# Diagonal blocks of short pairs transposed by the DMA, attention's steps at two places of a unit

## The chip, the cores and the metric

One core of one Trainium2 chip runs the whole program. The metric is the device time of one execution in microseconds (us), as the median of several runs. TensorE does the matmuls, VectorE (DVE) and ScalarE (ACT) the elementwise work, GpSimd (POOL) some scaling and subtraction, and SyncE (SP) issues the DMAs.

## What is computed

```python
# q, k, v: B, H, S, D = 4, 8, 576, 64; all fp32
scores = where(causal, -1e9, q @ k.T / sqrt(D))
local = softmax(scores) @ v
q_p = phi(q)                                  # where(q > 0, q, exp(q) - 1) + 1
mem_out = (q_p @ M_prev) / (q_p @ z_prev + 1e-6)
attn = g * mem_out + (1 - g) * local          # g = sigmoid(beta), one per head
x = attn as [2304 tokens, 512]
h = x @ w_in;  x = (h * sigmoid(1.702 * h)) @ w_out          # layer 0, d_ff = 2048
h = x @ w_in2; x = (h * clip(h + 3, 0, 6) / 6) @ w_out2      # layer 1
```

## The kernel before

Tokens are taken in six tiles of 384 (`TILES`). Four hold the first 384 rows of one batch ("long"), and two hold the last 192 rows of two batches each ("short"): the third and the sixth. Attention works on pairs of heads. A long tile has 4 pairs; a short one has 8, because it holds two batches. Pairs 0 to 7 belong to the first two tiles. From pair `CROSS` = 8 on (third tile and later) the softmax weights are transposed by the DMA and not by TensorE.

The mixture-of-experts layers (MoE) run as a stream of units, one for each of 16 blocks of d_ff. A unit has four quarters of h (`moe`, three matmuls of 384 columns each: L390, L392, L393) and then four quarters of y of the unit before (L361 to L363). So it has eight quarters, and after each the main loop counts `qi` up by one. While tile `ti` runs through layer 0, attention for tile `ti` + 1 is mixed in: attention is a generator, and `pump` (L1018; it is called at the end of the main loop) asks it for as many steps as the count allows. In h there is one PSUM bank (in layer 0), so a unit's first h matmul waits until the gate of the unit before (ACT at L327, DVE at L329) has read it.

A step of a short pair `i` is one of these: the first scores (`scores`, 2 banks), the memory term (`mem_read`, 1 bank), three steps of `turn(i - 1)`, the second scores "s4, s5" for rows 128 to 191 (2 banks), and `weigh(i - 1)`, which multiplies with v into o (1 bank). Attention has a rotation of three PSUM banks (`bank`). Scores go through a DVE minimum (L531), an ACT exponential (L536), a DVE reciprocal (L540) and a POOL scaling (L544). `over` then copies the weights as two 16-bit halves on ACT (L580), and SP issues a DMA transpose (L586) from `sp` to `xp`. `turn` starts `join`s: DVE copies (L605) that put the halves together into `pt`. The last 64 columns of a short pair, the diagonal block `t2`, are the exception: TensorE transposes them (t4b, L485), DVE copies the result from PSUM to `t4` (L705), and `weigh` reads `t4` last.

Instructions are put in order by a planner. It goes by what it believes to be ready, and by program order among those. `issue_after` ties an instruction behind another of its engine. The h matmuls are tied only behind attention's TensorE work of `SLACK` = 10 steps earlier. `later` lets a copy of `over` wait until a new gate's ACT cast has been written out, for up to `MOST` = 16 steps of the chains; at most two copies follow one gate.

The pace is `PG1` = 0.78: in a short tile 57 steps are spread over 0.78 * 128 quarters, one step every 1.75 quarters.

Of the kernel before, what the change touches and what calls it, by code (L numbers as in the profile page):

```python
# [11 lines left out]
U16 = mybir.dt.uint16  # L12
# [13 lines left out]
KQ = 39  # L26
CR = 8.5
OFF = 3
PG0 = (0.85, 0.8)
PG1 = 0.78  # L30
TB = 3
PB = 6
RB = 3
# [27 lines left out]
WAIT = (3, 5)  # L61
PB2, SB2, XB2, PTB2 = 4, 2, (4, 3), 2
APART = 2
MOST = 16
S2 = 104
SR = 8
CONV2 = tuple(range(4, 110, 13)) + tuple(range(140, 210, 10))
# [45 lines left out]
def attention_moe_kernel(ctx: ExitStack, tc: tile.TileContext, qk0, sk0, sk1, vm0, vm1, bb, w1, w2, out):  # L113
# [370 lines left out]
    def at_transpose(*args):  # L484
        on_pe[:] = [PE.transpose(*args).ins]  # L485

    def attention(ap, room, across):
# [84 lines left out]
        def over(i, a, src, n, blocks):  # L572
# [13 lines left out]
            SP.dma_start_transpose(out=turned, in_=halves[:, 0:2 * n])  # L586
            joins.setdefault(i, []).append((a, blocks, turned))

        def join(i, a, blocks, turned):

            yield
            t = heads(i)
            v = turned.rearrange("p (h b) q -> p h b q", h=2)
            if a is None:
                jobs = [(t[k][:, :, 128:192], v[:, :, :, 64 * k:64 * k + 64]) for k in range(2)]
            elif pairs[i][3] == 1:
                jobs = [(t[a][:, :, 0:128], v)]
            else:
                jobs = [
                    (t[a][:, to:to + 128 * (b1 - b0)].rearrange("p (b q) -> p b q", q=128), v[:, :, b0:b1])  # L600
                    for b0, b1, to in blocks
                ]
            for out, w in jobs:
                with tc.issue_after(gated["DVE"][-1]):
                    d = DVE.tensor_copy(out=out.bitcast(U16).rearrange("p b (q h) -> p h b q", h=2), in_=w)  # L605
                made.setdefault(i, {})[DVE] = d.ins

        def scores(i):

            ti, si, b, g, p, _ = pairs[i]  # L610
            norms[1] = ti
            q, k = qk[i]
            st = ap.tile([128, 12], F32, tag="st", name="st")
            mx, su = st[:, 0:6], st[:, 6:12]

            def product(banks, blocks):

                mm = in_a_run(free(banks[0]) + free(banks[1]))
                for o0, o1, c0 in blocks:
                    for a in range(2):  # L620
                        h = slice(64 * a, 64 * a + 64)
                        mm(
                            banks[a][:, o0:o1], lhsT=q[h, c0:c0 + 128], rhs=k[h, 0:o1 - o0], start=True, stop=True
                        )

            def soft(s, cols, dst, c):

                jobs = [(a, c0, c1, c + a * len(cols) + x) for a in range(2) for x, (c0, c1) in enumerate(cols)]
                yield
                for a, c0, c1, k in jobs:  # L630
                    masked_min(s[a][:, c0:c1], mask[:, 512 - (c1 - c0):512], BIG, mx[:, k:k + 1])
                yield
                for a, c0, c1, k in jobs:
                    d = expo(dst[a][:, c0:c1], s[a][:, c0:c1], mx[:, k:k + 1], su[:, k:k + 1])
                    if c1 == cols[-1][1]:
                        has_read(s[a], d)
                yield
                inverse(su[:, c:c + len(jobs)])
                yield
                for a, c0, c1, k in jobs:  # L640
                    norm(dst[a][:, c0:c1], su[:, k:k + 1], omg[:, 2 * p + a:2 * p + a + 1])
                if i >= CROSS:
                    yield
                    for a in range(2):
                        yield from over(i, a, dst[a], *merges0[g][c > 0])

            pp[i] = []
            if g == 0:
                parts = (((0, 128, 0), (128, 384, 128)), ((0, 384, 256),))
            else:  # L650
                parts = (((0, 512, 0),),)
            def weights(a):
                return room[0].tile([128, 512], F32, tag="p", bufs=PB2 if i >= CROSS else PB, name="p")

            t = [[None if i >= CROSS else weights(a) for _ in parts] for a in range(2)]
            pp[i] = [tuple(x) for x in t]
            c = 0
            for x, blocks in enumerate(parts):
                s = [bank("s") for _ in range(2)]
                if i >= CROSS:  # L660
                    for a in range(2):
                        t[a][x] = weights(a)
                product(s, blocks)
                start(("s", i, x), soft(s, [(o0, o1) for o0, o1, _ in blocks], [t[a][x] for a in range(2)], c))
                c += 2 * len(blocks)
                yield
            if g == 1:
                t = room[0].tile([128, 512], F32, tag="p", bufs=PB2 if i >= CROSS else PB, name="p4")
                t2 = ap.tile([128, 64], F32, tag="p5", name="p5")
                pp[i].append((t, t2))  # L670
                s, s2 = bank("s4"), bank("s5")
                mm = in_a_run(free(s) + free(s2))
                for o, c0, c1 in ((s, 0, 512), (s2[:, 0:64], 512, 576)):
                    for a in range(2):
                        h = slice(64 * a, 64 * a + 64)
                        mm(o[h], lhsT=q[h, 128:N1], rhs=k[h, c0:c1], start=True, stop=True)

                def soft4(s=s, s2=s2, t=t, t2=t2):
                    yield
                    masked_min(s, mask[:, 0:1].to_broadcast([128, 512]), BIG, mx[:, 2:3])  # L680
                    masked_min(s2[:, 0:64], mask4, mx[:, 2:3], mx[:, 3:4])
                    yield
                    has_read(s, expo(t, s, mx[:, 3:4], su[:, 2:3]))
                    has_read(s2, expo(t2, s2[:, 0:64], mx[:, 3:4], su[:, 3:4]))
                    yield
                    DVE.tensor_tensor(out=su[:, 2:3], in0=su[:, 2:3], in1=su[:, 3:4], op=ALU.add)
                    inverse(su[:, 2:3])
                    yield
                    norm(t, su[:, 2:3], omp[:, p:p + 1])
                    norm(t2, su[:, 2:3], omp[:, p:p + 1])  # L690
                    if i >= CROSS:
                        yield
                        yield from over(i, None, t, 512, [(0, 4, None)])

                start(("s", i, 2), soft4())
                yield
# [13 lines left out]
        def turn(i):  # L710
            ti, si, b, g, p, _ = pairs[i]
            if i >= CROSS:
                need(("s", i, 0), ("s", i, 1), ("s", i, 2))
                for k in (0, 1, None):
                    if k is not None:
                        head(i)
                    for n, (a, blocks, turned) in enumerate(joins[i]):
                        if a == k:
                            start(("j", i, n), join(i, a, blocks, turned))
                    if k == 1 and g == 1:  # L720
                        ps2 = bank("t4b")
                        at_transpose(ps2[0:64, 0:128], pp[i][2][1], ident)
                        start(
                            ("t", i, 0, 1),
                            evac(i, [(DVE, t4[0:64], ps2[0:64, 0:128].rearrange("p (a c) -> p a c", a=2), ps2)]),
                        )
                    yield
                if g == 0:
                    yield
# [100 lines left out]
        def weigh(i):  # L830

            ti, si, b, g, p, last = pairs[i]
            v = vm.pop(i)[0]
            need(*[("j", i, n) for n in range(4)])
            need(("t", i, 0, 0), ("t", i, 0, 1), ("t", i, 1, 0), ("t", i, 1, 1), ("m", i))
            t = pt.pop(i)
            o = bank("o")
# [111 lines left out]
        for i in range(CROSS, NPAIR):  # L949
            s = scores(i)  # L950
            if i == CROSS or pairs[i - 1][5]:
                yield from chunks(s, 1)
                yield from pause(2)
                yield from chunks(s, 9)
                begun(i)
            else:
                t, w = turn(i - 1), weigh(i - 1)
                yield from chunks(s, 1)
                yield from mem_read(i - 1)
                load_qk(i + 1)  # L960
                for gen, n in ((t, 1), (s, 1), (t, 1), (s, 9), (t, 9)):
                    yield from chunks(gen, n)
                begun(i)
                yield from chunks(w, 9)
            if pairs[i][5]:
                yield from pause(WAIT[pairs[i][3]])
                yield from mem_read(i)
                load_qk(i + 2)
                yield from ended(i, turn(i), weigh(i))


    with ExitStack():
# [80 lines left out]
        with tc.tile_pool(name="ap", bufs=2) as ap, ExitStack() as second, ExitStack() as third:  # L1053
# [28 lines left out]
            for layer, t, f in stream:  # L1082
# [8 lines left out]
                    convert_to(min(NF, PRE + 1 + int(qi / CR)))  # L1091
                if ti < 2 and 128 * ti + qi >= S2:
                    part_to(1 + (128 * ti + qi - S2) // SR)
                pump((qi - OFF) / (PG0[min(ti, 1)] * 128 / 36 if TILES[ti + 1][0][1] == 0 else PG1 * 128 / 57))

        with tc.tile_pool(name="x2p", bufs=2) as x2p:
            state["pool"] = x2p
# [68 lines left out]
```

## Time and profile before

| what | value |
|---|---|
| median of 3 runs | 1037.05 us (1036.7 to 1039.19) |
| the profiled execution | 1035.5 us |
| its span, first to last instruction | 1033.7 us |
| TensorE busy | 97% of the span |
| DVE, ACT, POOL busy | 49%, 53%, 30% |
| layer 0 of tile 2 with attention for the third tile (short) | 157.0 to 278.6 us |
| layer 0 of tile 3 with attention for the fourth tile (long) | 278.6 to 367.5 us |
| layer 0 of tile 5 with attention for the sixth tile (short) | 455.1 to 578.5 us |

The stage bounds are those of the copies of y at the end of each tile (L413). Engine times are busy times; a gap on TensorE of over 0.15 us counts as idle, and its releaser is inferred from the semaphores.

### The profile page before, as it was taken

How to read it: one execution, taken by the hardware profiler on the slowest of the kernel's cores; microseconds unless marked ns; L12 is line 12 of the kernel's file. 1: busy time of each engine (PE TensorE's matmuls, PEld its weight loads, DVE VectorE, ACT ScalarE, POOL GpSimd, SP SyncE). 2: the span in 40 equal slices, each digit the busy share in tenths (PEclk: the TensorE clock that was granted, in tenths of full speed). 3: DMA queues.
4: the chain of work that ended last, by engine and by line, in shares of the span. 5: the costliest groups of instructions: out<-in, count | busy, mean ns of one | idle time of the engine just before them, and what ended most of it. 6: DMA issues, size and time to landing. Idle time of an engine off the chain costs nothing.

```text
span 1033.7 us, 15855 instructions
## 1 busy us (share of the span) xinstructions
PE 999.3 (97%) x5737; PEld 884.3 (86%) x5737; DVE 507.1 (49%) x1263; ACT 552.7 (53%) x1142; POOL 309.8 (30%) x346
## 2 busy tenths in 40 slices
PE   7899999979999999999989999999999999999998
PEld 5556558767888888887868999999999999999998
DVE  6987775677554446346554887861121211211110
ACT  5877767656655365365554987963232332323322
POOL 3522013434344244233332331232222222222221
PEclk9999999999999999999999999999999999999999
DMA  5844418765454044236644774010010000100000
GB/s 176 308 160 166 155 62 204 183 154 125 119 95 97 16 111 82 70 77 124 123 97 101 298 272 145 1 31 32 1 62 1 31 31 1 47 16 1 32 1 31
DMA packets 110175, 99.15 MB, mean 96 GB/s; under 512 B 80400, under 2 KB 89616, under 8 KB 110096
## 3 DMA queue, kind: packets, MB, share of 16 engines
q1 hardware_dynamic: 110096, 98.14, 33.8%
q8 instruction: 45, 0.74, 0.3%
q14 instruction: 34, 0.28, 0.1%
HBM read 61.41 MB, written 9.44 MB: 69 GB/s over the span
## 4 chain that ended last, share of the span: by engine, by line
PE 67%; DVE 5%; DMA 4%; ACT 3%; issue 2%; POOL 1%; ACTq 0%; DVEq 0%; POOLq 0%; SPq 0%
PE h L390 11%; PE h L392 10%; PE h L393 10%; PE y L361 10%; PE y L363 10%; PE y L362 10%; DMA xp<-sp 3%; PE o L470 3%; PE s L470 2%; ACT p L536 1%; DVE pt L605 1%; DVE s L531 1%; ACT sp L580 1%; DVE w L274 1%; POOL p L544 1%
## 5 line engine op out<-in xcount | busy, mean ns | idle before, releaser
L341 POOL TENSOR_TENSOR g<-t,g 128x384 fp32r<-128x384 f32 x173 | 185.7, 1074 | 482.6 <-ACT g L338 369.5
L390 PE MATMUL h<-xs,w 128*128 128x384 f32 x704 | 243.1, 345 | 9.3 <-DVE t L329 9.1
L392 PE MATMUL h<-xs,w 128*128 128x384 f32 x704 | 236.9, 336 | 0.2 <-DVE w L274 0.2
L393 PE MATMUL h<-xs,w 128*128 128x384 f32 x704 | 236.7, 337 | 0.0
L361 PE MATMUL y<-g,w 128*128 128x384 f32 x704 | 236.5, 336 | 0.0
L362 PE MATMUL y<-g,w 128*128 128x384 f32 x704 | 236.2, 335 | 0.0
L363 PE MATMUL y<-g,w 128*128 128x384 f32 x704 | 221.2, 337 | 0.0
L333 DVE SCALAR_TENSOR_TENSOR t<-t,h 128x384 f32<-128x384 f32 x96 | 53.1, 553 | 278.6 <-ACT t L331 278.5
L544 POOL TENSOR_SCALAR p<-p,st,omg 128x128 f32<-128x128 f32 (+3 forms) x128 | 95.9, 760 | 198.4 <-DVE st L540 100.4
L390 PEld LDWEIGHTS h<-xs,w 128*128 128x128 f32 x704 | 132.7, 189 | 24.4 <-DVE t L329 12.3
L331 ACT ACTIVATE t<-h,three 128x384 f32<-128x384 f32 x96 | 55.8, 583 | 169.6 <-PE h L393 169.6
L338 ACT CAST g<-t 128x384 fp32r<-128x384 f32 x176 | 90.2, 513 | 93.1 <-DVE t L333 50.0
L361 PEld LDWEIGHTS y<-g,w 128*128 128x128 f32 x704 | 132.4, 188 | 2.6 <-issue 1.8
L392 PEld LDWEIGHTS h<-xs,w 128*128 128x128 f32 x704 | 133.0, 189 | 1.4 <-issue 0.8
L393 PEld LDWEIGHTS h<-xs,w 128*128 128x128 f32 x704 | 132.9, 189 | 0.8 <-issue 0.8
L363 PEld LDWEIGHTS y<-g,w 128*128 128x128 f32 x704 | 130.4, 188 | 3.2 <-issue 2.6
L362 PEld LDWEIGHTS y<-g,w 128*128 128x128 f32 x704 | 132.3, 188 | 1.0 <-issue 0.8
L536 ACT ACTIVATE p<-s,st 128x256 f32<-128x256 f32 (+4 forms) x160 | 82.3, 523 | 57.2 <-DVE st L531 54.4
L580 ACT COPY sp<-p 128x1024 uint16<-128x1024 uint16 (+1 forms) x80 | 75.2, 957 | 31.9 <-POOL p L544 25.3
L531 DVE CUSTOM_DVE_ANT_0 s<-s,mask 128x128 f32<-128x128 f32 (+3 forms) x144 | 72.4, 527 | 25.3 <-PE s L470 24.6
L605 DVE COPY pt<-xp 128x512 uint16<-128x512 uint16 (+3 forms) x112 | 60.6, 600 | 34.9 <-DMA xp<-sp 24.7
L329 DVE SCALAR_TENSOR_TENSOR t<-t,h 128x384 f32<-128x384 f32 x80 | 43.9, 550 | 68.4 <-ACT t L327 66.0
(79 smaller groups left out, 1111.5 us busy)
## 6 DMA issues: line engine op xcount, KB each, us to landing
r<-in_w_dram SPq DMA_DIRECT2D x64, 512.0 KB, 6.2
wt<-r SPq DMA_DIRECT2D x32, 256.0 KB, 2.6
vm<-in_vm_dram SPq DMA_DIRECT2D x16, 386.0 KB, 3.5
qk<-in_qk_dram SPq DMA_DIRECT2D x16, 384.0 KB, 3.5
qk<-in_sk_dram SPq DMA_DIRECT2D x32, 192.0 KB, 3.4
x2d<-yo SPq DMA_DIRECT2D x24, 192.0 KB, 2.0
xr<-x2d SPq DMA_DIRECT2D x24, 192.0 KB, 2.9
out_dram<-yo SPq DMA_DIRECT2D x24, 192.0 KB, 2.0
```

Of the source, the lines that this page charges most:

```text
L338: gated["ACT"].append(ACT.copy(out=g[:, 0], in_=t).ins)
L341: d = {"DVE": DVE, "POOL": POOL}[e].tensor_tensor(out=g[:, 1], in0=t, in1=f32(g[:, 0]), op=ALU.subtract)
L361: PE.matmul(ys[d], lhsT=w[:, 0, o:o + 128], rhs=g[:, 0], start=(f == 0), stop=False)
L362: PE.matmul(ys[d], lhsT=w[:, 1, o:o + 128], rhs=g[:, 0], start=False, stop=False)
L363: PE.matmul(ys[d], lhsT=w[:, 0, o:o + 128], rhs=g[:, 1], start=False, stop=(f == NF - 1))
L390: PE.matmul(h, lhsT=w[:, 0, c:c + 128], rhs=x[:, 0], start=first, stop=False)
L392: PE.matmul(h, lhsT=w[:, 1, c:c + 128], rhs=x[:, 0], start=False, stop=False)
L393: PE.matmul(h, lhsT=w[:, 0, c:c + 128], rhs=x[:, 1], start=False, stop=last)
L531: DVE.tensor_tensor_reduce(out=o, in0=o, in1=m, scale=-SCALE, scalar=init, op0=ALU.add, op1=ALU.min, accum_out=out)
L536: return ACT.activation(out=dst, in_=o, func=AF.Exp, scale=-1.0, bias=m, accum_out=s)
L544: (DVE, POOL)[e[norms[0] % len(e)]].tensor_scalar(out=dst, in0=dst, scalar1=s, scalar2=w, op0=ALU.mult, op1=ALU.mult)
L580: ACT.copy(out=halves[:, 0:2 * n].rearrange("p (h c) -> p h c", h=2), in_=src[:, 0:n].bitcast(U16).rearrange("p (c h) -> p h c", h=2),)
```

## The change

Three things change. The diagonal block of a short pair from the third tile on is copied on ACT and transposed by the DMA like the rest, and two DVE copies put it into `t4`; the TensorE transpose and its copy go for these pairs. From the second tile on, `pump` is called only where `qi` modulo 8 is 4 (behind h) or 0 (behind y), with a lead of 1 and 3 quarters added to the count. And the order of steps within a pair changes: both first steps of `turn` come ahead of the pair's second scores. `PG1` goes from 0.78 to 0.85 (a step every 1.91 quarters) and `MOST` from 16 to 3.

```diff
+PLACES = {0: 3, 4: 1}
-PG1 = 0.78
+PG1 = 0.85
-MOST = 16
+MOST = 3
+        def over_diagonal(i, src):
+            halves = room[0].tile([128, 128], U16, tag="sp5", bufs=1, name="sp5")
+            with tc.issue_after(gated["ACT"][-1]):
+                ACT.copy(
+                    out=halves.rearrange("p (h c) -> p h c", h=2),
+                    in_=src.bitcast(U16).rearrange("p (c h) -> p h c", h=2),
+                )
+            turned = room[0].tile([128, 128], U16, tag="xp5", bufs=1, name="xp5")
+            SP.dma_start_transpose(out=turned.rearrange("p (b q) -> p b q", q=128), in_=halves)
+            joins.setdefault(i, []).append((2, None, turned))
+
+        def join_diagonal(i, turned):
+            yield
+            words = t4[0:64].rearrange("p a c -> p (a c)").bitcast(U16).rearrange("p (q h) -> p h q", h=2)
+            for h in range(2):
+                d = DVE.tensor_copy(out=words[:, h], in_=turned[64 * h:64 * h + 64])
+                made.setdefault(i, {})[DVE] = d.ins
+
...
                     if i >= CROSS:
                         yield
                         yield from over(i, None, t, 512, [(0, 4, None)])
+                        over_diagonal(i, t2)
...
-                need(("s", i, 0), ("s", i, 1), ("s", i, 2))
+                need(("s", i, 0), ("s", i, 1))
                 for k in (0, 1, None):
+                    if k is None:
+                        need(("s", i, 2))
...
-                    if k == 1 and g == 1:
-                        ps2 = bank("t4b")
-                        at_transpose(ps2[0:64, 0:128], pp[i][2][1], ident)
-                        start(
-                            ("t", i, 0, 1),
-                            evac(i, [(DVE, t4[0:64], ps2[0:64, 0:128].rearrange("p (a c) -> p a c", a=2), ps2)]),
-                        )
+                        elif (a, k) == (2, None):
+                            start(("j", i, n), join_diagonal(i, turned))
...
-            need(*[("j", i, n) for n in range(4)])
+            need(*[("j", i, n) for n in range(5)])
...
-                for gen, n in ((t, 1), (s, 1), (t, 1), (s, 9), (t, 9)):
+                for gen, n in ((t, 1), (t, 1), (s, 1), (s, 9), (t, 9)):
...
-                pump((qi - OFF) / (PG0[min(ti, 1)] * 128 / 36 if TILES[ti + 1][0][1] == 0 else PG1 * 128 / 57))
+                ahead = 0 if ti == 0 else PLACES.get(qi % 8)
+                if ahead is not None:
+                    pump((qi + ahead - OFF) / (PG0[min(ti, 1)] * 128 / 36 if TILES[ti + 1][0][1] == 0 else PG1 * 128 / 57))
```

## Rows read from the trace of the kernel before

**Rows 1.** The page's first part: busy us, share of span, instructions.
```profile
PE 999.3 (97%) x5737; PEld 884.3 (86%) x5737; DVE 507.1 (49%) x1263; ACT 552.7 (53%) x1142; POOL 309.8 (30%) x346
```

**Rows 2.** Windows by stage: stretch, its length, each engine's busy us, clock, DMA.
```profile
157.00:278.56 121.56, 108.59 (x688) 89.48 (x687) 81.99 (x228) 77.78 (x169) 44.01 (x48) 0.99 0.65 155
278.56:367.45 88.89, 88.65 (x528) 77.89 (x527) 44.46 (x146) 46.62 (x114) 36.42 (x43) 1.00 0.35 78
...
455.11:578.47 123.36, 115.97 (x740) 99.87 (x739) 68.12 (x195) 69.47 (x141) 42.11 (x46) 0.99 0.55 128
...
705.00:771.80 66.80, 66.80 (x387) 66.80 (x386) 10.90 (x20) 21.20 (x41) 16.18 (x16) 1.00 0.08 26
```

**Rows 3.** Waits of TensorE, 157 to 279: total us, times, longest.
```profile
PE h L390 <- DVE t L329: 6.2, 7, 1.5
PE o L470 <- DVE t L705: 2.7, 2, 1.6
PE t4b L485 <- DVE mo L818: 2.6, 1, 2.6
PE s L470 <- ACT p L536: 1.2, 1, 1.2
```

**Rows 4.** Waits of TensorE, 455 to 579.
```profile
PE s L470 <- ACT p L536: 3.1, 3, 1.4
PE h L390 <- DVE t L329: 2.7, 2, 1.8
PE o L470 <- ACT p L536: 1.4, 1, 1.4
```

**Rows 5.** Groups by line and form, 157 to 579: busy us, mean ns, idle before.
```profile
L580 ACT COPY sp<-p 128x1024 uint16<-128x1024 uint16 x48 | 49.6, 1042 | 23.2 <-POOL p L544 20.0 <-DMA xp<-sp 3.1
...
L605 DVE COPY pt<-xp 128x512 uint16<-128x512 uint16 x48 | 21.4, 483 | 17.4 <-DMA xp<-sp 17.4
...
L485 PE MATMUL t4b<-ident,p 128*64 128x128 f32 x16 | 4.4, 275 | 2.8 <-DVE mo L818 2.8
L705 DVE COPY t<-t4b 64x128 f32<-64x128 f32 x16 | 4.4, 275 | 0.0
```

**Rows 6.** Timeline of TensorE round one t4b inside y: start, us, what.
```profile
478.20 0.34 PE L362 MATMUL y<-g,w 128*128 128x384 f32 x1
478.37 0.27 PE L485 MATMUL t4b<-ident,p 128*64 128x128 f32 x1
...
478.66 0.34 PE L361 MATMUL y<-g,w 128*128 128x384 f32 x1
```

**Rows 7.** Chain that ended last: start, length, engine, tile and line, instructions.
```profile
546.19 1.12 PE s L470 x8
...
561.29 1.78 PE o L470 x22
```

**Rows 8.** Window of one stretch at a lower granted clock (third last column).
```profile
228.90:232.30 3.40, 3.40 (x12) 3.40 (x12) 2.89 (x9) 2.26 (x7) 1.26 (x2) 0.50 0.64 143
```

**Rows 9.** Timeline of TensorE round one visit of attention's scores.
```profile
403.35 0.34 PE L363 MATMUL y<-g,w 128*128 128x384 f32 x1
403.62 0.70 PE L470 MATMUL s<-qk 64*128 64x256 f32 x4
404.25 0.44 PE L361 MATMUL y<-g,w 128*128 128x384 f32 x1
404.53 0.34 PE L362 MATMUL y<-g,w 128*128 128x384 f32 x1
```

**Rows 10.** Tile xp, 157 to 279, and its landing times, 455 to 579.
```profile
L586 SPq DMA_TRANSPOSE xp<-sp x24: 1231/1276/2339, 160.5 to 261.8; - x24
...
  DVE pt L605: 8.1, 7
...
DMA to landing us min/median/max: 3.0/3.3/4.7
```

**Rows 11.** Timeline of DVE: a join that waits for the DMA.
```profile
164.98 0.74 DVE L605 COPY pt<-xp 128x1024 uint16<-128x1024 uint16 x1 [1.76 <-DMA xp<-sp]
```

## The prediction

> **What bounds the kernel now.** I read the page's first part, then the window table by stage, then who waits on TensorE, then the timeline round the transposes that the change removes. TensorE is busy 97% of the span [rows 1], so an edit pays only where it shortens TensorE's own queue. The window table says where that can be: a tile with no attention beside it takes about 66.8 us and TensorE is never idle there, and a stage that carries long pairs is 88.9 us long with 0.2 us idle. The two stages that carry short pairs (the mixture-of-experts part, MoE, of the second tile with attention for the third, and of the fifth with attention for the sixth) are 121.6 and 123.4 us long and idle 13.0 and 7.4 us [rows 2]. Those 20.4 us are what can be won by order alone. The lists of waits name them. In the first of the two, 6.2 us are the first h matmul of a unit waiting for the DVE half of the gate (one PSUM bank holds h, so the next unit's h waits until the gate has read it), 2.7 us are o waiting for the DVE copy of the transposed diagonal, 2.6 us are that transpose waiting for a bank that the memory term still holds, 1.2 us are scores waiting for a bank that an exponential still reads [rows 3]. In the second they are 2.7 us for the gate, 3.1 us scores and 1.4 us o behind exponentials [rows 4].
>
> **The sum is made against the profiled execution's 1035.5 us** (span 1033.7). The median of the runs shown is 1037.05, 1.55 more; I add that at the end.
>
> **a. The removed transpose.** In each of 16 short pairs one matmul t4b goes, and its DVE copy [rows 5]. Its own row says 0.27 us, but much of that overlaps: round one in the middle of y, two y slots take 478.66 - 478.20 = 0.46 us instead of 2 x 0.17 [rows 6]. That is 0.12 us a piece, 16 x 0.12 = 1.9 us. Ends: 0, and 16 x 0.27 = 4.3. I take -1.9, from the row in which nothing waits.
>
> **b. The waits attached to it.** t4b took a seventh bank in each pair of a rotation of three, so each pair's banks fell differently; with six the memory term always gets the third bank and the scores the first two. Gone with it: t4b behind the memory term 2.8 [rows 5], o behind the copy of t4b 2.7 [rows 3], o behind an exponential 1.4 [rows 4], together -6.9. What takes their place: o now needs two DVE copies from the DMA's result. I went through the steps by hand with the new pace: the last joins (k = None) and the weighing fall at one place in 3 of the 8 pairs of a short tile, and are half a unit or more apart in the others. In those 3, two copies of 0.48 us [rows 5] and two small ones, which I bound by L705's 0.28 us [rows 5], stand ahead of o: 1.5 us, of which the planner (it lists an instruction when it believes it ready) can cover some with h. 6 pairs x 0.5 us gives +3, ends 0 and +9.
>
> **c. The gate's wait.** Before, a step came every 1.75 quarters, so half of attention's TensorE work fell inside h and half between two h; now all of it lies between one h's end and the next one's start. Per unit 8 / 1.91 = 4.2 steps instead of 2.3 stand there. A short pair's TensorE work is about 4.5 us (o 1.8 and each of two score steps 1.1 [rows 7]; about 0.5 for the memory term's four small matmuls, an estimate) in 7 steps, 0.65 us a step, so the gate gets 1.9 x 0.65 = 1.2 us more. The 9 waits of 8.9 us in all [rows 3, 4] average 1.0. I take two thirds, -6; ends 0 (the cause is a full DVE or ACT queue, and that stays) and -8.9.
>
> **d. Scores behind exponentials**, 1.2 + 3.1 us [rows 3, 4]: with the rotation of b, four steps lie between two users of a bank at one end and three at the other. Half, -2.1; ends 0 and -4.3.
>
> **e. The clock.** Twice in these stages TensorE's granted clock falls to 0.50 for one stretch of 3.4 us (1.2 instead of 2.4 GHz), at 228.9 [rows 8] and alike at 522.4, and both stretches come just behind the largest waits of b and c. Each costs 1.7 us. I take one of them, -1.7; ends 0 and -3.4.
>
> **f. Fewer changes between the two kinds of work.** A visit of attention to TensorE costs about 0.2 us beside its own matmuls: the last MoE start before it is followed after 0.27 us instead of 0.17, and the first after it after 0.28 instead of 0.17 [rows 9]. By the code, steps with TensorE work stand at 40 places of a short tile and 16 of a long one, and then at 21 and 14: at most 42 visits less in four tiles, 8.4 us. But the planner already puts many side by side, so I take -1.8.
>
> **g. What is added.** Per short pair: one ACT copy of 128 columns, an eighth of the 1.04 us one [rows 5], estimated 0.3 us with its fixed part; one DMA transpose more on SP's queue, bounded above by the 1.24 us that a large one holds that queue and the 3.0 to 4.7 us to landing that large ones show [rows 5, 10]; two small DVE copies for the one removed. ACT and DVE are busy 78 and 82 of 121.6 us there [rows 2], and hide 5 us each; ahead of a gate a copy delays it by its length: +1, ends 0 and +4. Queued behind the new transpose on SP are the loads of later pairs' q, k, v and, in the first short stage, of weights to be split; they are issued pairs ahead, nothing. That score rows are copied after 3 steps of waiting at most, instead of 16, starts the transposes earlier; ACT then has a 1.04 us copy ahead of a gate more often, which is in the +4. At the stage's end, the last memory term and weighing, before some 7 quarters apart, now come at one place: at most the 2.6 us that t4b once waited for the memory term [rows 3], twice; covered in part by h of the last unit, +2, ends 0 and +5.
>
> A rule speaks against this change: the Trainium skill, page VectorE: DVE Perf Modes, section Rules for kernel authors, says to transpose 128x128 on TensorE where PSUM will do and through the DMA only otherwise, and its section The three transpose paths gives 390 ns against 1309 ns. Rows 5 and 10 agree on the order (0.27 us against 3 us or more). By that rule the sum would lose 16 x 0.9 = 15 us, an estimate from that page; it holds only if the latency is on the path, which is the first rival below.
>
> **Sum:** -1.9 - 6.9 + 3 - 6 - 2.1 - 1.7 - 1.8 + 1 + 2 = -14.4. 1035.5 - 14.4 + 1.55 = 1022.7 us.
>
> **Rivals.** *Slower: DVE's queue held by joins.* DVE takes its instructions in order; a join whose data is late holds the gate behind it, and the next h behind that. It happens already: joins waited 8.1 us in the first short stage [rows 10], and the one at 164.98 held DVE for 1.76 us [rows 11] and then h for 1.5, the longest in rows 3. The change moves the last score step of a pair one step nearer to its joins (7 steps of 1.91 instead of 9 of 1.75 quarters: 2.4 quarters, 1.2 us, less) and puts a second transpose behind the large one (1.24 us of issue). Against it: the transposes also start earlier, and the planner can place joins later. At 1.8 us in 12 of 16 pairs it is +21.6, with a and the whole of b +12.8: 1049.9 us. It decides from about 5 pairs of 16 on. *The places don't hold:* h is tied only to attention ten steps back, so the planner may spread the steps again and c, d and f stay away: a, b and e, -7.5, 1029.5 us. For it: already now the trace's order is not that of the code everywhere. *Nothing left:* a and b are won, and the gate behind ACT's earlier copies and the fuller end of the stage give back the upper ends of g (4 + 5): about 1037 us.
>
> **Chances.** Forecast 0.55, places don't hold 0.2, nothing left 0.12, slower 0.13. A measurement of this kernel can tell 0.3% (3 us) from no change. The forecast's own ends are some 12 us to either side (all of b to f won, or c, d and e nearly lost). The range, 1011 to 1038, leaves out the slower rival and a little at the bottom. Faster by over 0.3%: 0.75; within: 0.12; slower: 0.13.
>
> **What would show it.** The trace of after should have no t4b; o's wait should not name a DVE copy from the DMA for more than 3 us in all; h behind the gate should fall below 4 us over both stages; at most one stretch at half clock between 157 and 580 us; the two short stages about 7 us shorter each and the long ones 1 us or less. If joins waiting for xp hold DVE for over 20 us and h's wait grows, the first rival is right. If the order of visits still shows steps inside h, the second is.

## The result and the profile after

The changed kernel is slower: 1041.53 us median (1040.26 to 1044.84, 8 runs) against 1036.10 us (1034.0 to 1039.19, 8 runs of before beside them), a ratio of 1.0051 with a 95% interval of 1.0036 to 1.0065. Forecast was 1022.7 us.

The page's first part of the kernel after, and its group for a unit's first h matmul (busy us, mean ns of one, idle time just before it and what ended that). L391 is L390 of before, L330 is L329, and so on; the new lines are L594 (ACT copy of the diagonal), L599 (its transpose) and L607 (its join).

```profile
PE 1003.1 (97%) x5721; PEld 884.8 (85%) x5721; DVE 511.7 (49%) x1279; ACT 553.8 (53%) x1158; POOL 303.9 (29%) x346
...
L391 PE MATMUL h<-xs,w 128*128 128x384 f32 x704 | 242.1, 344 | 14.5 <-DVE t L330 14.1
```

The t4b matmuls are gone (16 matmuls fewer than in [rows 1]). But h now waits 14.1 us for the DVE half of the gate (13.5 of it in the two short stages), where the forecast had it fall below 4. The windows by stage, to be read beside [rows 2]:

```profile
157.00:277.90 120.90, 107.06 (x671) 87.44 (x670) 84.96 (x230) 74.35 (x170) 37.38 (x43) 0.99 0.65 155
277.90:371.90 94.00, 93.95 (x545) 81.33 (x543) 45.43 (x152) 50.79 (x128) 37.59 (x47) 1.00 0.34 76
371.90:463.60 91.70, 90.35 (x519) 77.31 (x518) 41.55 (x131) 45.32 (x106) 35.47 (x40) 1.00 0.35 81
463.60:582.90 119.30, 111.65 (x705) 95.83 (x706) 69.75 (x197) 67.81 (x145) 40.53 (x44) 0.99 0.54 128
```

From 157.0 to the end of the second short stage it is 425.9 us, against 421.5 before (578.47 - 157.00). TensorE's idle time in it is 22.9 us; before it was 20.6. The stages must not be compared one by one, since matmuls have moved over their bounds: the first long one now holds 545 against 528, and the second short one 705 against 740, of which the t4b account for 8.

To take the stages' contents out, I went through the starts of all TensorE matmuls of the four tiles with attention, from the first h of the second tile on and over the same 1548 MoE matmuls in both, and took 0.172 us off for each MoE matmul. What is left are visits of attention, and gaps between two MoE matmuls with no visit between them. Visits took 128.3 us before and take 120.9 now, in 91 and 80 visits; the gaps were 19.8 and are 33.9. So the visits gave 7.4 us, and 14.1 us went to the gaps. Idle time explains most of both: in the visits it fell from 17.8 to 8.8 us, and in the gaps, where nothing of attention stands between, it rose from 2.8 to 13.8. The waits have for the most part moved, from attention's matmuls to MoE's.

Waits of TensorE in the first short stage after (total, times, longest):

```profile
PE h L391 <- DVE t L330: 9.5, 7, 2.1
PE o L471 <- DVE mo L837: 1.5, 2, 1.1
PE o L471 <- DVE t L607: 1.4, 1, 1.4
PE s L471 <- ACT p L537: 1.0, 2, 0.7
```

and in the second:

```profile
PE h L391 <- DVE t L330: 4.0, 4, 1.6
PE o L471 <- DVE mo L837: 1.6, 1, 1.6
PE y L362 <- ACT yo L414: 1.6, 1, 1.6
PE s L471 <- ACT p L537: 1.2, 2, 0.8
```

Against [rows 3, 4], the waits that hung on t4b are gone, and scores behind exponentials halved. But o waits for the memory term and for the new join, and h behind the gate went from 8.9 to 13.5 us. The longest of these, at 232.7, in the timeline of the kernel after (all times in us). ACT:

```profile
229.74 0.51 ACT L328 ACTIVATE t<-h 128x384 f32<-128x384 f32 x1
```

DVE, with the idle time before an instruction and what ended it in brackets:

```profile
230.43 0.16 DVE L541 RECIPROCAL st<-st 128x1 f32<-128x1 f32 x1
233.62 0.74 DVE L626 COPY pt<-xp 128x1024 uint16<-128x1024 uint16 x1 [3.03 <-DMA xp<-sp]
234.25 0.53 DVE L330 SCALAR_TENSOR_TENSOR t<-t,h 128x384 f32<-128x384 f32 x1
```

SP's queue:

```profile
229.32 1.25 SPq L587 DMA_TRANSPOSE xp<-sp  x1
231.01 0.35 SPq L156 DMA_DIRECT2D vm<-in_vm_dram  x1
```

And TensorE:

```profile
234.84 0.44 PE L391 MATMUL h<-xs,w 128*128 128x384 f32 x1 [2.12 <-DVE t L330]
```

ACT had its half of the gate done at 230.25. DVE stood from 230.6 to 233.6 before a join whose transpose was issued at 229.32, and the gate's second half came only behind that join. The next h started at 234.84. This is the mechanism of the slower rival. But the join is a large one, which the kernel before has too; it waits for no transpose of the diagonal.

The diagonal's own join stands in front of the gate in this way at only one of h's waits, and that one is 1.6 us long:

```profile
504.80 1.25 SPq L587 DMA_TRANSPOSE xp<-sp  x1
506.15 1.17 SPq L599 DMA_TRANSPOSE xp<-sp  x1
508.45 0.48 DVE L607 COPY t<-xp 64x128 uint16<-64x128 uint16 x2 [3.98 <-DMA xp<-sp]
508.96 0.56 DVE L330 SCALAR_TENSOR_TENSOR t<-t,h 128x384 f32<-128x384 f32 x1
509.57 0.44 PE L391 MATMUL h<-xs,w 128*128 128x384 f32 x1 [1.63 <-DVE t L330]
```

DVE stood before this join from 504.47, and its transpose was issued only at 506.15. Not all waits of h in the four tiles are of this kind. In the kernel after, 8.1 of the 14.1 us have a join that waited for the DMA between ACT's half of the gate and DVE's; in the kernel before it is 4.4 of 9.1. At nearly all the others ACT's half itself came late. ACT's copies of the weights now wait longer for POOL, over the four tiles (before, then after):

```profile
ACT sp L580 <- POOL p L544: 25.3, 24, 2.7
ACT sp L581 <- POOL p L545: 45.6, 28, 4.6
```

### The profile page after: what moved, and what is told of

Its sections match the earlier page's. It is cut to its first block, busy times and chain, and to the rows that moved or that the text cites. A ratio compares the mean times of both kernels' runs of the same rounds, so it can differ in the third digit from the quotient of the medians.

```text
span 1038.8 us, 15891 instructions
## 1 busy us (share of the span) xinstructions
PE 1003.1 (97%) x5721; PEld 884.8 (85%) x5721; DVE 511.7 (49%) x1279; ACT 553.8 (53%) x1158; POOL 303.9 (29%) x346
## 4 chain that ended last, share of the span: by engine, by line
PE 46%; DMA 2%; DVE 2%; issue 2%; ACT 1%; POOL 1%; DVEq 0%; POOLq 0%
PE y L364 8%; PE y L362 8%; PE y L363 8%; PE h L391 8%; PE h L394 8%; PE h L393 8%; DMA xp<-sp 2%; POOL p L545 1%; ACT p L537 0%; DVE s L532 0%; DVE pt L626 0%; DVE t L330 0%; ACT sp L581 0%; PE o L471 0%; DVE t L607 0%
## 5 line engine op out<-in xcount | busy, mean ns | idle before, releaser
L391 PE MATMUL h<-xs,w 128*128 128x384 f32 x704 | 242.1, 344 | 14.5 <-DVE t L330 14.1
L391 PEld LDWEIGHTS h<-xs,w 128*128 128x128 f32 x704 | 132.9, 189 | 26.2 <-DVE t L330 19.0
L545 POOL TENSOR_SCALAR p<-p,st,omg 128x128 f32<-128x128 f32 (+3 forms) x128 | 92.2, 732 | 186.0 <-DVE st L541 97.3
L532 DVE CUSTOM_DVE_ANT_0 s<-s,mask 128x128 f32<-128x128 f32 (+3 forms) x144 | 72.3, 527 | 29.2 <-PE s L471 28.4
L330 DVE SCALAR_TENSOR_TENSOR t<-t,h 128x384 f32<-128x384 f32 x80 | 43.8, 549 | 69.3 <-ACT t L328 65.2
L471 PE MATMUL s<-qk 64*128 64x256 f32 (+5 forms) x384 | 70.6, 455 | 5.3 <-ACT p L537 4.8
```

The lines of the kernel that those rows point to most:

```text
L391: PE.matmul(h, lhsT=w[:, 0, c:c + 128], rhs=x[:, 0], start=first, stop=False)
L532: DVE.tensor_tensor_reduce(out=o, in0=o, in1=m, scale=-SCALE, scalar=init, op0=ALU.add, op1=ALU.min, accum_out=out)
L545: (DVE, POOL)[e[norms[0] % len(e)]].tensor_scalar(out=dst, in0=dst, scalar1=s, scalar2=w, op0=ALU.mult, op1=ALU.mult)
```

## The experiments

Ratios are to the kernel before, run beside each on the same chip, with their 95% intervals. Where two experiments are set against each other, it is by these ratios, which come from different chips.

**The parts one at a time.** First each part alone or undone.

Diagonal by the DMA alone: the kernel before with `over_diagonal`, `join_diagonal` and their calls put in, and t4b taken out (a few of its lines, as in the diffs below with dots).

```diff
+                        over_diagonal(i, t2)
...
-                    if k == 1 and g == 1:
-                        ps2 = bank("t4b")
...
+                        elif (a, k) == (2, None):
+                            start(("j", i, n), join_diagonal(i, turned))
```

> The kernel before with one part of the change alone: the diagonal blocks go through the DMA; places, pace, order of steps and MOST stay. Theory A (joins hold DVE: a fourth transposed piece makes the last join late, DVE stands in order, the gate and the next h wait behind it): about 4 us slower than before, 1.004, with more h waiting for the gate. Theory B (the two places are what costs: the planner takes attention out from between y and h, so nothing covers the gate): t4b and its waits go at no price, about 5 us faster, 0.995.

Measured: 0.9991 (0.9979 to 1.0003), no change. Neither theory. In the trace the waits that hung on t4b are gone (5.5 us), and h waits 12.0 us for the gate over the four tiles, where it was 9.1 before. That a gain and a price cancel fits this, but isn't shown.

The places alone, in the kernel before:

```diff
+PLACES = {0: 3, 4: 1}
-PG1 = 0.78
+PG1 = 0.85
...
+                ahead = 0 if ti == 0 else PLACES.get(qi % 8)
+                if ahead is not None:
...
```

> The kernel before with the two places and PG1 0.85 alone; t4b, order of steps and MOST = 16 stay. Theory A: within 2 us of before, since no transpose is added. Theory B: 5 to 8 us slower, 1.005 to 1.008, with the loss in y followed by h with no visit between.

Measured: 0.9986 (0.9973 to 1.0000), no loss. Theory B (the places themselves cost) falls for the places alone.

The places undone, in the changed kernel:

```diff
-PG1 = 0.85
+PG1 = 0.78
...
-                ahead = 0 if ti == 0 else PLACES.get(qi % 8)
-                if ahead is not None:
...
```

> The changed kernel with pump at every quarter again and PG1 0.78; diagonal by the DMA, order of steps and MOST = 3 stay. Theory A: still 4 to 5 us slower than before (1.004 to 1.005). Theory B: 3 to 5 us faster than before (0.995 to 0.997).

Measured: 1.0043 (1.0029 to 1.0058), as slow as the change. What is left in it is the diagonal, the order of steps and `MOST` = 3. But it isn't slow in the same way. h waits for the gate about as long as before:

```profile
PE h L390 <- DVE t L329: 9.3, 9, 3.1
```

Its mean granted clock over the runs is 0.989, against 0.993 in the kernel before beside it, and 0.004 of 1036 us is up to 4.4 us, an estimate: about all that it loses. So this run doesn't say that the places have no part in h's longer wait.

`MOST` undone, in the changed kernel:

```diff
-MOST = 3
+MOST = 16
```

> The changed kernel with MOST back at 16. If copies that come earlier on ACT and hold the gate there are the cause (a third theory, C): 3 to 5 us faster than the changed kernel, at or below before. Theories A and B: the transposes start later, so no gain, the changed kernel's 1.005 or 1 to 3 us more.

Measured: 1.0064 (1.0044 to 1.0084). Not the cause within the change.

**The order of steps.** It was the part not yet tried, and the prediction had given it no term. Undone in the changed kernel:

```diff
-                for gen, n in ((t, 1), (t, 1), (s, 1), (s, 9), (t, 9)):
+                for gen, n in ((t, 1), (s, 1), (t, 1), (s, 9), (t, 9)):
```

> The changed kernel with the order of steps of before (first step of the turn, second scores, second step), everything else as changed. Theory D (the order: second scores behind both first steps of the turn stand beside the last joins and o, so their DVE minima and the joins fill DVE ahead of the gate): 0.995 to 0.998 of before, 7 to 9 us faster than the changed kernel, and MoE waits with no visit between fall to before's 10 and 6 us in the short stages. If it is the sum of the diagonal by the DMA and the places that costs (theory E, each alone was harmless): still 1.004 to 1.006.

Measured: 1.0101 (1.0084 to 1.0117): 5 us slower than the change. Theory D falls here; within the change the new order helps. The converse is the new order alone in the kernel before (the same two lines the other way):

> The kernel before with the new order of steps alone; t4b, pump at every quarter, PG1 0.78 and MOST = 16 stay. Theory D: 1.004 to 1.006, 4 to 6 us slower. Theory E: within 2 us of before.

Measured: 1.0035 (1.0022 to 1.0048), 3.6 us slower. So the same edit costs in one kernel and pays in the other. Its longest waits of TensorE over the four tiles:

```profile
PE s L470 <- DVE mo L818: 6.2, 4, 2.8
PE s L470 <- DVE st L539: 5.5, 2, 3.2
PE h L390 <- DVE t L329: 3.8, 5, 1.3
```

The scores wait for the bank of the memory term, which before they never did [rows 3, 4]: with t4b as seventh bank in a rotation of three, the second scores fall on other banks when they change places with it. With six banks, in the changed kernel, this line is absent. It names what is new, but not the price: TensorE is idle for 20.1 us in these tiles, and for 20.6 in the kernel before. What the trace has more of is half clock, 13.6 us against 6.8 in these tiles, which is 3.4 us of TensorE's work. The mean granted clock of its runs is 0.990, against 0.992 beside it.

The old order in short pairs only, in the changed kernel:

```diff
-                for gen, n in ((t, 1), (t, 1), (s, 1), (s, 9), (t, 9)):
+                for gen, n in (((t, 1), (s, 1), (t, 1), (s, 9), (t, 9)) if pairs[i][3] == 1 else ((t, 1), (t, 1), (s, 1), (s, 9), (t, 9))):
```

> The changed kernel with the old order of steps in short pairs only; long pairs keep the new one. Theory D as told (it acts through a short pair's second scores): as e5, 0.995 to 0.999. If the order costs in the long stages: 1.003 or more.

Measured: 1.0130 (1.0115 to 1.0145). No less than the full undoing (1.0101): it acts through the short pairs.

The turn asks for all three chains of scores at once again, in the changed kernel:

```diff
-                need(("s", i, 0), ("s", i, 1))
+                need(("s", i, 0), ("s", i, 1), ("s", i, 2))
                 for k in (0, 1, None):
-                    if k is None:
-                        need(("s", i, 2))
```

> The changed kernel, in which the turn again asks for all three chains of scores before its first step and not for the third only ahead of the last joins (the order of steps stays changed). If writing out the third chain's copies and transposes later is the cause: 4 us or more faster than the changed kernel. Theories D and E: 1.004 to 1.006, as the changed kernel.

Measured: 1.0052 (1.0037 to 1.0066). No part in it.

`MOST` = 3 alone, in the kernel before:

```diff
-MOST = 16
+MOST = 3
```

> The kernel before with MOST = 3 alone. Theory C (copies that come earlier on ACT stand ahead of the gate and wait there for GpSimd): 3 to 8 us slower, 1.003 to 1.008. Theory A (joins that wait for the DMA hold DVE): no slower, 0.996 to 1.001, since transposes start earlier.

Measured: 1.0032 (1.0017 to 1.0046), 3.3 us slower, in the range of theory C. Its mechanism doesn't show: ACT's copies wait 24.8 us for GpSimd over the four tiles, against 25.3 before. The joins wait less for the DMA, as theory A has it (13.7 against 24.7 us), and h waits more for the gate (12.3 against 9.1), but TensorE's idle time is the same (20.3 against 20.6 us). The mean granted clock of its runs is 0.990, against 0.993 beside it, which is up to 3.2 us, an estimate. Within the change `MOST` = 3 cost nothing that can be told (above).

The diagonal by the DMA and the places together, old order, `MOST` = 16 (the diffs of the first two):

> The kernel before with the diagonal by the DMA and the two places with PG1 0.85; old order of steps and MOST = 16. Theory C: 0.995 to 0.999, the best so far, since MOST is out. If the two parts clash with each other (theory E): 1.004 to 1.008.

Measured: 1.0058 (1.0038 to 1.0078). Each alone did no harm, together they cost 6 us. The DVE waits over the four tiles of this kernel:

```profile
DVE pt L626 <- DMA xp<-sp: 25.6, 18, 3.0
...
DVE t L607 <- DMA xp<-sp: 14.5, 5, 4.5
```

and of the kernel with the diagonal alone:

```profile
DVE pt L625 <- DMA xp<-sp: 29.9, 25, 3.0
...
DVE t L606 <- DMA xp<-sp: 4.6, 3, 1.8
```

The new join, a copy of 0.25 us, holds DVE for 14.5 us in five places in the first and for 4.6 us in three places in the second.

**The joins' dependence on the DMA.** All joins of the changed kernel copy from a constant:

```diff
-            v = turned.rearrange("p (h b) q -> p h b q", h=2)
+            v = mask.bitcast(U16)[:, 0:128 * turned.shape[1]].rearrange("p (h b q) -> p h b q", h=2, q=128)
-                d = DVE.tensor_copy(out=words[:, h], in_=turned[64 * h:64 * h + 64])
+                d = DVE.tensor_copy(out=words[:, h], in_=mask.bitcast(U16)[64 * h:64 * h + 64, 0:128])
```

> The changed kernel, whose joins copy from a constant tile in place of the DMA's result (same shapes, same count; the transposes are still made, the softmax weights that reach the product with v are not the right ones). No join can wait for a transpose. Theory A: at least 5 us faster than the changed kernel, 0.999 of before or less. Theory C: within 3 us of the changed kernel, 1.003 to 1.006.

Measured: 0.9915 (0.9887 to 0.9942), 14 us faster than the change. And in the kernel before (the first two lines):

> The same exchange of the joins' source in the kernel before (its weights, too, are then not the right ones). Theory A: faster than before by some 3 us, less than what the changed kernel gains. Theory C: within 2 us of before, or faster by as much as the changed kernel gains.

Measured: 0.9850 (0.9828 to 0.9872), 15 us faster than before. The waits of h behind the gate over these tiles, in the changed kernel with constant joins:

```profile
PE h L391 <- DVE t L330: 1.3, 3, 0.6
```

and in the kernel before with them:

```profile
PE h L390 <- DVE t L329: 1.5, 4, 0.7
```

This is half of what theory A said. In both kernels nearly all of h's wait for the gate goes when the joins no longer depend on the DMA (from 9.1 to 1.5 us in the kernel before, from 14.1 to 1.3 in the changed one). But taking the dependence away gains as much in the kernel before as in the changed one, and the changed one stays 7 us behind. So the joins as a whole don't explain the difference; the new one may.

Only the diagonal's join copies from the constant, first with the diagonal and the places alone:

```diff
-                d = DVE.tensor_copy(out=words[:, h], in_=turned[64 * h:64 * h + 64])
+                d = DVE.tensor_copy(out=words[:, h], in_=mask.bitcast(U16)[64 * h:64 * h + 64, 0:128])
```

> Diagonal by the DMA and the two places as in the run of both (1.0058), but the diagonal's two join copies read a constant tile, so that they never wait for their transpose (which is still made; t4 then does not hold the right weights). If DVE held by the diagonal's join is the clash: 0.996 to 1.000, the 13.1 us of DVE waiting for it gone. If it is not: 1.004 to 1.007.

Measured: 1.0021 (1.0007 to 1.0035). 3.8 us of the 6 come back, not all. And the same two lines in the changed kernel:

> The changed kernel with the same exchange for the diagonal's join alone (t4 does not hold the right weights). If the diagonal's join is what costs in the change too: 0.998 to 1.001, most of the 5 us back. If ACT's copies (MOST) and the order cost: 1.003 to 1.005.

Measured: 0.9941 (0.9925 to 0.9957), 11.4 us faster than the change and 6 us faster than before. With the large joins free as well it was 0.9915 (above), only 2.7 us more. Its wait of h over the four tiles:

```profile
PE h L391 <- DVE t L330: 6.0, 7, 2.6
```

and its DVE waits for the DMA there:

```profile
DVE pt L626 <- DMA xp<-sp: 14.5, 11, 3.3
```

The changed kernel over the same stretch, the wait of h:

```profile
PE h L391 <- DVE t L330: 14.1, 13, 2.1
```

and its DVE waits for the DMA:

```profile
DVE pt L626 <- DMA xp<-sp: 24.2, 21, 3.1
...
DVE t L607 <- DMA xp<-sp: 5.7, 2, 4.0
```

With the one small join free, DVE waits 15.4 us less for the DMA (14.5 against 29.9) and h 8 us less for the gate. Only 5.7 of the 15.4 carry the small join's own name; the large joins' waits shrink with it. That goes beyond the wait itself: the planner also orders the instructions otherwise when the join depends on nothing. The first short stage shows it: the small join never waits there in the changed kernel (its 5.7 us lie in the second), DVE's wait for the DMA even grows when it is freed, from 11.8 to 13.6 us, and still h's wait falls from 9.5 to 5.0. How much of the 11.4 us is waiting and how much is order, this run can't separate. Part of it is the clock: its mean over the runs is 0.997, against 0.993 for the change.

**A remedy, and the diagonal left out.** The diagonal's transpose ahead of the large one, in the changed kernel:

```diff
+                        over_diagonal(i, t2)
                         yield from over(i, None, t, 512, [(0, 4, None)])
-                        over_diagonal(i, t2)
```

> The changed kernel with the diagonal's copy and transpose ahead of the large transpose of the same chain, so that it is issued and lands first. If it was late because it stood last: most of the 11 us that its join cost come back, 0.995 to 0.999 of before. If DVE then waits for the large one's join in its place: 1.001 to 1.006, the wait only changes its name.

Measured: 1.0058 (1.0039 to 1.0078), no gain. Its DVE waits in the second short stage:

```profile
DVE t L607 <- DMA xp<-sp: 10.2, 4, 4.0
```

The join still waits, more than in the change (5.7). But the exchange hardly reached SP's queue. In 12 of 16 pairs (14 in the change) the small transpose is still the last of the pair's four to be issued, as at the longest wait:

```profile
504.13 1.24 SPq L587 DMA_TRANSPOSE xp<-sp  x1
505.47 1.17 SPq L599 DMA_TRANSPOSE xp<-sp  x1
507.77 0.48 DVE L607 COPY t<-xp 64x128 uint16<-64x128 uint16 x2 [3.96 <-DMA xp<-sp]
```

So the run doesn't settle whether its place behind the large one makes it late. What the trace does show is that the join stands too early in DVE's order here: DVE waits for it from 503.81, before either transpose is issued. In the large one's place it would have landed some 1.3 us earlier, an estimate from the two issues, and DVE would still have stood for 2.6 us.

The diagonal back on TensorE, all other parts of the change kept:

```diff
-                        over_diagonal(i, t2)
...
-                    if k is None:
+                    if k is None or (k == 1 and g == 1):
                         need(("s", i, 2))
...
+                    if k == 1 and g == 1:
+                        ps2 = bank("t4b")
...
```

> The changed kernel with the diagonal on TensorE again (places, pace, new order of steps and MOST = 3 stay; the third chain is asked for ahead of the second step of the turn). If the diagonal's part is what makes the change slow: 0.994 to 0.999, and a version that beats both. If MOST and the order cost as much as they did alone (0.3% each): 1.003 to 1.006.

Measured: 0.9980 (0.9965 to 0.9995): 2 us faster than before and 7.4 us faster than the change, the lowest ratio of the kernels that keep the whole computation, though the places alone (0.9986) can't be told from it. Its h waits 9.5 us for the gate over the four tiles:

```profile
PE h L391 <- DVE t L330: 9.5, 11, 1.5
```

**More distance to the joins.** Second scores ahead of both steps of the turn, in the kernel before, and then with the places as well:

```diff
-                for gen, n in ((t, 1), (s, 1), (t, 1), (s, 9), (t, 9)):
+                for gen, n in ((s, 1), (t, 1), (t, 1), (s, 9), (t, 9)):
```

> The kernel before with a pair's second scores ahead of both first steps of the turn (second scores, first, second, against first, second scores, second), so one step more between scores and joins. If the distance to the joins is what is short: 2 to 4 us faster, 0.996 to 0.998, the mirror of the new order alone (1.0035). If the planner's order merely scatters: within 4 us either way.

Measured: 1.0025 (1.0014 to 1.0036).

> The two places with PG1 0.85 and the second scores first; t4b and MOST = 16 as before. With more distance: 0.994 to 0.997, faster than both kernels. If the order merely scatters: 0.997 to 1.004.

Measured: 0.9999 (0.9983 to 1.0015). Neither is faster, so the theory of the distance falls, and both lie where a mere scatter of the planner's order would put them. That is a warning: moving the second scores one step later costs 0.35% in the kernel before, and one step earlier costs 0.25%. Each edit makes the planner deal out all queues anew, and a quarter to a third of a per cent either way need not have a reason of its own.

## Why the prediction was wrong, point by point

**What failed first: the replacement in b.** The prediction saw the waits at t4b go (-6.9) and priced what takes their place at +3, ends 0 and +9: the joins' copies ahead of o. Measured within the change, the join's dependence on the DMA costs 11.4 us (1.0051 against 0.9941), outside even the upper end. The error was where it looked: at o, which reads the join, and not at what stands behind the join in DVE's order. o waits 1.4 us for L607; h waits 14.1 for the gate. How the small join comes to cost so much is shown only in part. The trace has it waiting directly in front of the gate for 1.6 us of h's wait. How the rest comes about, by the order that the planner makes round it or by the clock, stays open.

**a and the gain of b were forecast with the right sign, at about twice their size.** With the diagonal off TensorE and its join free, against the diagonal on TensorE, the kernel gains 0.9980 - 0.9941, 4.0 us, with the planner's new order in it. The forecast had -1.9 - 6.9 for it, -8.8. Together with the price the diagonal's part is 7.4 us to the bad (1.0051 against 0.9980), where -5.8 was forecast (with the +3). That alone is 13 of the 20 us between forecast and result.

**c did not come.** -6 was forecast, and h's wait grew by 4.6 us (8.9 to 13.5). It had counted on all of attention standing between y and the next h. In the trace the visits that stand there fell from 49 to 37, where those between two h fell only from 12 to 7. Units such as those at 193.6 and 232.3 have none there, because the planner had put it inside y. The gate also became later: the mean time from the end of h to ACT's half rose from 0.8 to 1.8 us in the second tile and from 1.4 to 1.7 in the fifth, and from the end of ACT's half to the start of DVE's from 0.7 to 1.1 and from 0.3 to 0.7. The forecast had taken a third off for "a full DVE or ACT queue stays"; the queue got fuller in front of the gate. With the diagonal's join free, h waits 6.0 us, 3.1 less than before, about half of c.

**d and f came.** Scores behind exponentials fell from 4.3 to 2.2 us (-2.1 forecast), visits from 91 to 80, which at 0.2 us is 2.2 (1.8 forecast).

**e did not.** Two stretches at half clock are there again, the first behind h's wait of 2.1 us at 193.9, the second behind 1.6 us of y waiting for its bank and 0.9 us of h:

```profile
196.60:200.00 3.40, 3.40 (x13) 2.98 (x14) 3.27 (x12) 2.25 (x7) 1.01 (x1) 0.51 0.68 167
466.30:469.70 3.40, 3.40 (x12) 3.40 (x12) 2.17 (x5) 2.35 (x4) 2.55 (x3) 0.50 0.31 61
```

**The order of steps had no term,** and `MOST` stood only in the upper end of g. Alone they cost 3.6 and 3.3 us. All parts but the diagonal together gave 2 us (0.9980), where c to g, with the order counted as nothing, summed to -8.6 (the +1 in g belongs to the diagonal).

**The first rival named the mechanism best, at the wrong odds.** It named the join, the queue, the gate and the next h, and got 0.13. That chain stands in the trace for 8.1 of h's 14.1 us, most of it before large joins. Its price was too high: 1049.9 us, where 1041.5 was measured. Two more details in it were off. The distance from the second scores to their last joins falls from nine steps to eight, not to seven, so from 15.8 to 15.3 quarters. And its sign of over 20 us of DVE waiting for xp as a mark of the change was no mark: before already waits 22.9 us in the two short stages, the changed kernel 28.4. The wait was large in the kernel before and the joins' dependence on the DMA cost 15 us there, order included, as the run with constant joins shows; the prediction read 8.1 us of it [rows 10] and set it down as something that happens, not as what stands behind most of [rows 3].

**The third rival came near in number.** *Nothing left* gave about 1037 us, but its sum leaves out the +3 of b; with it, it is 1040.3 us, close to the 1041.5. Its reason, the gate behind ACT's earlier copies, is not shown: ACT's half is late at most of h's other waits, but `MOST` undone in the change gained nothing.

**The rule that spoke against the change** held in the changed kernel. The Trainium skill, page VectorE: DVE Perf Modes, section Rules for kernel authors, would have left the 128x128 transpose on TensorE, and here that is 7.4 us faster. In the kernel before, the same exchange alone made no difference (0.9991). The figures that the prediction took from the page, 390 against 1309 ns, do not show up as 16 equal losses: DVE waited for only two of the 16 small transposes.

**Open.** With no join waiting for the DMA, the changed kernel is still 7 us behind the kernel before with the same edit (0.9915 against 0.9850). `MOST` and the order, which cost 3 us each alone, could be that, but no run tried them there. Nor is it settled why the planner puts the diagonal's join before its data; that it believes the small transpose to be quicker than it is would fit, and was not tried.

## What to carry to other kernels

When work moves from an engine to the DMA, price the instruction that consumes the result by everything queued behind it on its own engine, not by its own length or by its reader. In a kernel whose order is made by a planner, try each part of a change alone and undone: here two parts that were harmless alone cost 6 us together, and a third cost 3.6 us in one kernel and paid 5 in the other. Look in the trace whether an edit reached the queue that it was meant for: one here, the small transpose put first, mostly did not. And before building on a wait that the profile shows, take it away once with a constant: that would have shown that 15 us lay in the joins before the change, though the planner's order changes with it.

## What the runs showed of the hardware

A transpose with an eighth of the data saves little time. The line of the diagonal's transpose in the changed kernel, SP's queue time and its landing:

```profile
L599 SPq DMA_TRANSPOSE xp<-sp x16: 1124/1177/2253, 164.9 to 561.4; - x16
...
DMA to landing us min/median/max: 2.3/2.3/3.7
```

In the median it holds SP's queue for 1.18 us, where the large one held it for 1.28 in the first short stage before [rows 10], and it lands after 2.3 us, where the large one took 3.3 in the second. The copies round it were as small as estimated, 0.29 us on ACT and 0.25 on DVE:

```profile
L607 DVE COPY t<-xp 64x128 uint16<-64x128 uint16 x32 | 8.0, 251 | 6.0 <-DMA xp<-sp 5.7
...
L594 ACT COPY sp<-p 128x128 uint16<-128x128 uint16 x16 | 4.7, 294 | 0.0
```

The granted clock is part of such small differences. Its mean over a profiled execution was 0.995 in the kernels before and after, but 0.985 with the places undone and 0.988 with the second scores first; 0.01 of it over some 1040 us is up to 10 us of TensorE's work, an estimate. Three of the losses of 3 to 5 us above (the places undone, the new order alone, `MOST` alone) come with a mean clock that is lower by 0.002 to 0.004 over their runs, and with at most 0.7 us more idle time on TensorE in the four tiles. Why the clock falls more in these kernels, no run was made to find out.
